# Multiplying keys by bf16 pairs on VectorE, with moved evictions and a split last zero write, in a decode-attention gradient kernel

## The chip, the cores and the metric

The kernel runs on one core of one Trainium2 chip. The metric is device time in microseconds (us) of one execution, and the figure for a kernel is the median over its runs. Engines are named as the profile names them: PE is the matrix engine, PEld its weight load, DVE the vector engine, ACT the scalar engine, POOL the GpSimd engine, and SP the engine that issues most transfers. PEclk is the clock that was granted to PE, as a share of full speed. A program on one core has no other core to compare with, so a run counts as slow only when it is more than 1.5% above the fastest run of the same kernel.

## The reference, cut to what matters

The reference is one decode step of a transformer block, forward, and the gradients of it with respect to the input, both caches and all weights. There are two sequences (B = 2), one new token each, 32 query heads on 8 key/value heads (REP = 4 query heads share one), head size 128, and caches of 32,768 rows. Attention looks at the last W = 4096 rows only.

```python
def _A_ref(x, k_cache, v_cache, wq, wo):
    ...
    W = min(4096, max(256, Sk // 4))                 # 4096 of 32768
    q = (x @ wq) ...                                 # 32 heads of 128
    k = jnp.repeat(k_cache[:, :, Sk - W:, :], rep, axis=1)
    v = jnp.repeat(v_cache[:, :, Sk - W:, :], rep, axis=1)
    scores = jnp.einsum("bhqd,bhkd->bhqk", q, k) * (Dh ** -0.5)
    p = _softmax(scores, axis=-1)
    return jnp.einsum("bhqk,bhkd->bhqd", p, v) ... @ wo

h  = x + _A_ref(_layernorm(x), ...)
h2 = h + (gelu(ln2 @ w_gate) * (ln2 @ w_up)) @ w_down      # ln2 = _layernorm(h)
# returned: h2 and the gradients for x, k_cache, v_cache, wq, wo, w_gate, w_up, w_down
```

What matters for the time: the gradients of the two caches have the caches' full shape, and 28,672 rows of each (sequence, head) are zero. These are 32 regions of 7.34 MB, 234.9 MB of zeros that have to be written. Everything else that the kernel loads and stores is 96.7 MB.

## The kernel before: the parts that count

All zero writes are issued at the start on POOL's own transfer queue, from one tile of zeros. They run behind everything else for most of the program.

```python
ZE = 1024
zt = const.tile([P, ZE], U8)
zero_regions = [o[b, g, 0:Z, :].rearrange("r d -> (r d)")
                for o in (out_2, out_3) for b in range(B) for g in range(HKV)]

def zero_cast(i):                                     # 7.34 MB, rows of 4 KB
    nper = (Z * DH // 2) // (P * ZE)
    nc.gpsimd.dma_start(out=zero_regions[i].bitcast(F32).rearrange("(p k e) -> p k e", p=P, k=nper),
                        in_=zt[:].unsqueeze(1).to_broadcast([P, nper, ZE]))
# ...
for i in range(len(zero_regions)):
    zero_cast(i)
```

`attention(b)` treats the eight heads of one sequence in turn. Its rows of keys K and values V lie on 128 partitions, 32 rows (NJ) of 128 on each. Per head it transposes K on PE and evicts the transposes from PSUM (`kt_unit`), makes the scores, the exponentials `ef` (`softmax`), and then, in eight units of four rows (`m_unit`), the products of each key row with its four exponentials. PE multiplies these products `pk` with V into `M_ps`, which the gradient of the scores needs later. `finish` copies the head's other sums out of PSUM: the copy into `oPK` on DVE marks the end of a head in the trace.

```python
def evac(out, in_):                                   # alternates DVE and ACT
    ...

def kt_unit(g, u):
    ...                                               # 8 transposes of K into KT_ps on PE
    evac(KT[:], KT_ps[:])
    return KT

def softmax(g):
    ...
    ef = stA.tile([P, NJ, REP], F32, tag="ef", name="ef")
    nc.vector.tensor_tensor(out=ef[:], in0=S[:], in1=negm[:]..., op=ALU.add)
    nc.scalar.activation(out=ef[:], in_=ef[:], func=ACT.Exp)
    Ef[g] = ef
    ...

def m_unit(g, u, M_ps):
    pk = at(PK_OFF[b][u % n_pk], [P, pk_j, REP, DH], BF16, "pK")
    ef, Kb = Ef[g], Kt[b, g]
    j0 = u * pk_j
    for (n, h0, h1) in ((pk_j, 0, 2), (pk_j - 1, 2, 3)):              # 1024 and 384 elements on DVE
        shape = [P, n, h1 - h0, DH]
        nc.vector.tensor_tensor(out=pk[:, 0:n, h0:h1, :], in0=Kb[:, j0:j0 + n, :].unsqueeze(2).to_broadcast(shape),
                                in1=ef[:, j0:j0 + n, h0:h1].unsqueeze(3).to_broadcast(shape), op=ALU.mult)
    for (jj, i) in [(jj, 3) for jj in range(pk_j)] + [(pk_j - 1, 2)]: # 5 x 128 elements on ACT
        nc.scalar.activation(out=pk[:, jj, i, :], in_=Kb[:, j0 + jj, :], func=ACT.Copy, scale=ef[:, j0 + jj, i:i + 1])
    ...                                               # oPK_ps and M_ps matmuls

def finish(g, M_ps):
    oPK = stA.tile([P, 2, DH], F32, tag="oPK", name="oPK", bufs=1)
    nc.vector.tensor_copy(out=oPK[:], in_=oPK_ps[:])
    ...
```

The order of the whole program is attention(0), the FFN and score gradients of sequence 0, attention(1), the same for sequence 1, the weight gradients, and last the tail: the used rows of the cache gradients are outer products. Each group is made by PE into `ps_g`, evicted in turn by DVE and ACT, and stored in pieces of 1 MB on SP's queue.

```python
for n, (b, what) in enumerate(jobs):                  # dV and dK of each sequence
    for gq in range(2):
        ...
        for jp in range(8):
            for ap in range(2):
                ps = ps_G.tile([P, 2, 4 * DH], F32, tag="ps_g", name="ps_g")
                ...                                   # two matmuls
                for a in range(2):
                    evac(st_vs[a][:, ap * 2:(ap + 1) * 2, :, jp, :], ps_v[:, :, a * 2:(a + 1) * 2, :])
        for a in range(2):
            for b2 in range(2):
                nc.sync.dma_start(out=dst_v[:, b, gq * 4 + a * 2 + b2, :, :], in_=sts[a][:, b2, :, :])
```

## Time and profile before

The time before is 820.84 us (five runs, 819.89 to 821.32). The span of the profiled run is 819.7 us, from its first to its last instruction.

| what | before |
|---|---|
| time, median | 820.84 us |
| DVE, ACT, PE busy over the span | 62%, 54%, 72% |
| zeros written (queue q0), everything else (q1) | 234.88 MB, 96.74 MB |
| first and last eviction of the tail | 701.2 and 806.6 us |
| last packet of zeros | 734.5 us |
| zero bytes still to write when the tail begins | 1.95 MB |

Here are lines of the profile page of the kernel before: the span, the busy time of each engine in us, its share of the span and its number of instructions; the span in 40 equal slices of 20.5 us, where a digit is the busy share of a slice in tenths and the last row is the DMA rate in GB/s; and the software queue that writes the zeros with its packets, megabytes and share.

```profile
span 819.7 us, 13311 instructions
PE 591.9 (72%) x5316; PEld 325.4 (40%) x5350; DVE 509.4 (62%) x893; ACT 443.1 (54%) x1016; POOL 35.9 (4%) x49
...
DVE  2899799603252323979484851435646637999993
ACT  1898789403333423979484731333644434576683
...
GB/s 364 415 419 420 421 422 422 423 425 423 423 423 422 418 416 426 421 421 422 423 422 424 424 423 424 423 423 422 428 416 424 425 425 427 351 295 279 387 275 341
...
q0 software_dynamic: 57856, 234.88, 86.1%
```

No engine of the core is busy all the time, and the DMA row tells why that is not the whole matter: for 33 slices (2 to 34) it stands at 415 to 428 GB/s. Only in the last six does it drop, to 351 down to 275. So the program has two parts. Up to about 697 us the transfers run flat out, whatever the compute does; after that the transfers wait for compute. The share of busy time averaged over the span says nothing about either part.

Three stretches of the table of busy time show what compute does in them. The columns are the stretch in us, its length, then the busy time and the count of each engine, the granted clock, the DMA share and the DMA rate. The first stretch is one from attention(0), the others are from the end of the tail.

```profile
core 0: us, PE busy (x) PEld busy (x) DVE busy (x) ACT busy (x) POOL busy (x), PEclk, DMA share, GB/s
41.00:61.50 20.50, 17.81 (x238) 10.62 (x239) 19.98 (x33) 20.01 (x62) 0.00 (x0) 1.00 1.18 420
758.50:779.00 20.50, 14.27 (x44) 4.76 (x45) 19.02 (x27) 12.84 (x22) 0.00 (x0) 0.84 0.93 383
779.00:799.50 20.50, 17.11 (x59) 5.69 (x59) 18.68 (x31) 16.99 (x30) 0.00 (x0) 0.99 0.67 278
```

In attention(0) DVE and ACT are both full (19.98 and 20.01 us of 20.5). In the tail DVE is nearly full with evictions and the DMA runs at 278 GB/s: it has room. What fills the two engines in attention is in the list of groups, kept apart by shape. The columns are the line, engine, operation, output and input with their sizes, the count, busy time in us, the mean of one in ns, and the idle time before them with what ended it.

```profile
L377 ACT ACTIVATE mem<-mem,ef 128x128 bf16<-128x128 bf16 x640 | 200.0, 390 | 22.1 <-PE M_ps L388 16.9 <-remote 2.4 <-ACT mem L377 1.0
L374 DVE TENSOR_TENSOR mem<-mem,ef 128x1024 bf16<-128x1024 bf16 x128 | 154.8, 1209 | 17.5 <-PE M_ps L388 17.3
L374 DVE TENSOR_TENSOR mem<-mem,ef 128x384 bf16<-128x384 bf16 x128 | 69.3, 541 | 0.0
```

The two DVE sizes give a line: (1209 - 541) / (1024 - 384) = 1.044 ns per element, and 1209 - 1024 x 1.044 leaves about 140 ns of fixed cost. The exponentials are read as 32-bit floats.

Attention(1) looks different. The chain of work that ended last is followed back from the end. These three of its lines are its longest waits for transfers (start in us, length in us, what):

```profile
388.55 29.02 DMA mem<-in_A_v_cache_dram
...
433.83 31.34 DMA mem<-in_A_v_cache_dram
...
474.84 31.37 DMA mem<-in_B_w_down_dram
```

The last heads of attention(1) wait for loads of V that land some 30 us after they are issued, and the FFN then waits for w_down.

### The profile page before, as it was taken

What the parts mean: (1) busy time and instruction counts of PE and PEld (TensorE: products, weight loads), DVE (VectorE), ACT (ScalarE), POOL (GpSimd) and SP (SyncE); (2) the same over time, 40 slices, a digit from 0 to 9 for tenths busy, and PEclk for the clock granted to TensorE, in tenths of its full rate; (3) what the DMA queues carried; (4) which work ended last, traced back from release to release, by engine and by line L of the source; (5) the groups of instructions that cost most, each with busy time, mean ns of one, the idle gap of its engine ahead of it and who ended that gap; (6) DMA issues with size and microseconds to landing.
All of it is one profiled execution on the core that took longest, in us unless ns stands there. A gap on an engine that the chain in (4) does not pass through costs nothing.

```text
span 819.7 us, 13311 instructions
## 1 busy us (share of the span) xinstructions
PE 591.9 (72%) x5316; PEld 325.4 (40%) x5350; DVE 509.4 (62%) x893; ACT 443.1 (54%) x1016; POOL 35.9 (4%) x49
## 2 busy tenths in 40 slices
PE   3787877718977845877474776887988597776682
PEld 3554443307566633444242334474433142222220
DVE  2899799603252323979484851435646637999993
ACT  1898789403333423979484731333644434576683
POOL 4100000001000000000000000000000000000000
PEclk9999999965866975989796895956965586888897
DMA  9999999999999999999999999999999999976968
GB/s 364 415 419 420 421 422 422 423 425 423 423 423 422 418 416 426 421 421 422 423 422 424 424 423 424 423 423 422 428 416 424 425 425 427 351 295 279 387 275 341
DMA packets 69462, 332.48 MB, mean 406 GB/s; under 512 B 1804, under 2 KB 1816, under 8 KB 59288
## 3 DMA queue, kind: packets, MB, share of 16 engines
q0 software_dynamic: 57856, 234.88, 86.1%
q1 hardware_dynamic: 11532, 96.74, 49.3%
q8 instruction: 42, 0.69, 0.3%
q10 hardware_dynamic: 12, 0.01, 0.2%
q14 instruction: 20, 0.16, 0.1%
HBM read 49.29 MB, written 282.33 MB: 405 GB/s over the span
## 4 chain that ended last, share of the span: by engine, by line
PE 25%; DVE 12%; DMA 11%; ACT 5%; issue 2%; ACTq 0%; DVEq 0%; SPq 0%
DMA mem<-in_A_v_cache_dram 7%; PE ps_g L774 5%; DVE mem L88 4%; ACT mem L90 4%; DMA mem<-in_B_w_down_dram 4%; PE ps_gr L665 4%; PE ps_tb L225 4%; PE VT_ps L596 3%; DVE mem L374 2%; PE dP_ps L605 2%; PE M_ps L388 2%; DVE mem L253 2%; DVE mem L685 2%; PE ps_gq L745 1%; PE d_ln_ps L722 1%
## 5 line engine op out<-in xcount | busy, mean ns | idle before, releaser
L374 DVE TENSOR_TENSOR mem<-mem,ef 128x1024 bf16<-128x1024 bf16 (+1 forms) x256 | 213.7, 875 | 17.5 <-PE M_ps L388 17.3
L377 ACT ACTIVATE mem<-mem,ef 128x128 bf16<-128x128 bf16 x640 | 200.0, 390 | 22.1 <-PE M_ps L388 16.9
L388 PE MATMUL M_ps<-mem 128*128 128x512 bf16 x498 | 139.8, 397 | 36.0 <-DVE mem L374 29.7
L90 ACT COPY mem<-ps_tb 128x512 bf16<-128x512 bf16 x83 | 48.5, 585 | 127.0 <-PE ps_tb L225 73.3
L225 PE MATMUL ps_tb<-ident_bf,mem 128*128 128x128 bf16 x664 | 81.5, 266 | 25.1 <-DMA mem<-in_B_w_down_dram 16.9
L774 PE MATMUL ps_g<-mem 128*128 128x512 bf16 x250 | 80.6, 422 | 25.7 <-ACT mem L90 23.8
L88 DVE COPY mem<-ps_tb 128x512 bf16<-128x512 bf16 x83 | 35.2, 424 | 94.6 <-PE ps_tb L225 61.1
L90 ACT CAST mem<-ps_g 128x512 bf16<-128x512 f32 x128 | 74.7, 585 | 32.2 <-DVE mem L88 30.0
L88 DVE CAST mem<-ps_g 128x512 bf16<-128x512 f32 x128 | 82.6, 687 | 8.3 <-PE ps_g L774 6.5
L388 PEld LDWEIGHTS <-mem 128*128 128x128 bf16 x512 | 42.9, 100 | 97.2 <-DVE mem L374 54.0
L225 PEld LDWEIGHTS <-mem 128*128 128x128 bf16 x664 | 55.4, 129 | 51.2 <-issue 29.2
L332 PE MATMUL KT_ps<-ident_bf,mem 128*128 128x128 bf16 x512 | 47.0, 244 | 29.9 <-DMA mem<-in_A_k_cache_dram 19.7
L90 ACT COPY mem<-KT_ps 128x1024 bf16<-128x1024 bf16 x32 | 32.0, 1001 | 58.1 <-PE KT_ps L332 58.1
L774 PEld LDWEIGHTS <-mem 128*128 128x128 bf16 x256 | 26.7, 105 | 79.0 <-issue 65.4
L104 POOL DMA_DIRECT2D out_dram<-zt x32 | 33.7, 1143 | 517.3 <-DMA out_dram<-zt 505.9
L90 ACT COPY mem<-VT_ps 128x1024 bf16<-128x1024 bf16 x33 | 34.0, 1031 | 35.2 <-PE VT_ps L596 26.7
L332 PEld LDWEIGHTS <-mem 128*128 128x128 bf16 x512 | 36.7, 109 | 41.3 <-DMA mem<-in_A_k_cache_dram 20.2
L596 PE MATMUL VT_ps<-ident_bf,mem 128*128 128x128 bf16 x512 | 47.1, 244 | 1.6 <-DVE pkT L572 0.9
L596 PEld LDWEIGHTS <-mem 128*128 128x128 bf16 x512 | 37.9, 110 | 25.0 <-issue 17.7
L382 PE MATMUL oPK_ps<-mem 128*4 128x128 bf16 x512 | 28.7, 232 | 22.8 <-DMA mem<-in_A_v_cache_dram 22.8
L605 PE MATMUL dP_ps<-mem 128*128 128x512 bf16 x114 | 41.4, 437 | 4.8 <-ACT mem L90 4.8
L88 DVE CAST mem<-ps_gr 128x512 bf16<-128x512 f32 (+1 forms) x40 | 26.7, 671 | 28.6 <-PE ps_gr L665 28.4
(196 smaller groups left out, 628.2 us busy)
## 6 DMA issues: line engine op xcount, KB each, us to landing
out_dram<-zt POOLq DMA_DIRECT2D x32, 7168.0 KB, 163.3
out_dram<-mem SPq DMA_DIRECT2D x36, 1024.0 KB, 10.1
mem<-in_A_k_cache_dram SPq DMA_DIRECT2D x16, 1024.0 KB, 17.5
mem<-in_A_v_cache_dram SPq DMA_DIRECT2D x16, 1024.0 KB, 29.2
out_dram<-mem SPq DMA_DIRECT2D x5, 1792.0 KB, 25.1
mem<-in_A_wq_dram SPq DMA_DIRECT2D x1, 4096.0 KB, 12.5
mem<-in_A_wo_dram SPq DMA_DIRECT2D x1, 4096.0 KB
mem<-in_B_w_down_dram SPq DMA_DIRECT2D x2, 1792.0 KB, 27.3
```

The source lines that it names most:

```text
L88: nc.vector.tensor_copy(out=out, in_=in_)
L90: nc.scalar.copy(out=out, in_=in_)
L104: nc.gpsimd.dma_start(out=zero_regions[i].bitcast(F32).rearrange("(p k e) -> p k e", p=P, k=nper), in_=zt[:].unsqueeze(1).to_broadcast([P, ...
L225: nc.tensor.transpose(out=ps[:, a, :], in_=src_block(a), identity=ident_bf[:])
L332: nc.tensor.transpose(out=KT_ps[:, jj, :], in_=Kt[b, g][:, u * 8 + jj, :], identity=ident_bf[:])
L374: nc.vector.tensor_tensor(out=pk[:, 0:n, h0:h1, :], in0=Kb[:, j0:j0 + n, :].unsqueeze(2).to_broadcast(shape), in1=ef[:, j0:j0 + n, h0:h1]. ...
L377: nc.scalar.activation(out=pk[:, jj, i, :], in_=Kb[:, j0 + jj, :], func=ACT.Copy, scale=ef[:, j0 + jj, i:i + 1])
L388: nc.tensor.matmul(out=M_ps[:], lhsT=Vt[b, g][:, j, :], rhs=pk[:, jj, :, :].rearrange("p i d -> p (i d)"), start=(j == 0), stop=(j == NJ - 1))
L596: nc.tensor.transpose(out=VT_ps[:, jj, :], in_=Vt[b, g][:, a * 8 + jj, :], identity=ident_bf[:])
L605: nc.tensor.matmul(out=dP_ps[:, c, :], lhsT=dOpad[:, w0:w0 + P], rhs=VT[:, c * 4:(c + 1) * 4, :].rearrange("d a k -> d (a k)"), start=(i = ...
L665: nc.tensor.matmul(out=ps[:, :n], lhsT=lhsT_fn(k), rhs=rhs_fn(k), start=True, stop=True)
L774: nc.tensor.matmul(out=ps[:, a2, :], lhsT=lhs_bf[:, jp * P:(jp + 1) * P], rhs=rhs_bd[:, ap * 2 + a2, gq * 4:(gq + 1) * 4, :].rearrange("q ...
```

## The change

The change was meant to relieve DVE and ACT in attention. It has five parts.

1. In `m_unit` four DVE multiplies of 512 elements replace the two DVE multiplies and the five ACT multiplies. The exponentials are first written as bf16, each twice, so that all three operands are bf16 and are read in pairs of neighbouring elements.
2. ACT takes all evictions of the transposed K, which DVE and ACT shared before.
3. `ef` has one buffer instead of two, and the matmuls for `oPK_ps` are done with V for all four rows, then with K.
4. Small row tiles move: a pool is removed, `x` is loaded again when needed, the residual is added by four small matmuls instead of one, and a selector exists at partition 64 too. This is left out of the diff below.
5. The last zero region is written by three transfers (116 x 3, 128 x 11 and 12 x 3 rows of 4 KB) instead of one.

```diff
+    def zero_cast4(i):
+        ch = zero_regions[i].bitcast(F32).rearrange("(c e) -> c e", e=ZE)
+        c0 = 0
+        for n, k in ((116, 3), (P, 11), (12, 3)):
+            nc.gpsimd.dma_start(out=ch[c0:c0 + n * k, :].rearrange("(p k) e -> p k e", k=k),
+                                in_=zt[0:n, :].unsqueeze(1).to_broadcast([n, k, ZE]))
+            c0 += n * k
...
     for i in range(len(zero_regions)):
-        zero_cast(i)
+        (zero_cast if i < len(zero_regions) - 1 else zero_cast4)(i)
...                                        # in kt_unit
-                evac(KT[:], KT_ps[:])
+                nc.scalar.copy(out=KT[:], in_=KT_ps[:])
...                                        # in softmax
-                ef = stA.tile([P, NJ, REP], F32, tag="ef", name="ef")
+                ef = stA.tile([P, NJ, REP], F32, tag="ef", name="ef", bufs=1)
+                ee = stA.tile([P, NJ, REP, 2], BF16, tag="ee", name="ee")
...
-                Ef[g] = ef
+                nc.vector.tensor_copy(out=ee[:], in_=ef[:].unsqueeze(3).to_broadcast([P, NJ, REP, 2]))
+                Ef[g] = ee
...                                        # in m_unit
-                for (n, h0, h1) in ((pk_j, 0, 2), (pk_j - 1, 2, 3)):
-                    shape = [P, n, h1 - h0, DH]
-                    nc.vector.tensor_tensor(out=pk[:, 0:n, h0:h1, :], in0=Kb[:, j0:j0 + n, :]..., in1=ef[...]..., op=ALU.mult)
-                for (jj, i) in [(jj, 3) for jj in range(pk_j)] + [(pk_j - 1, 2)]:
-                    nc.scalar.activation(out=pk[:, jj, i, :], in_=Kb[:, j0 + jj, :], func=ACT.Copy, scale=ef[...])
+                shape = [P, pk_j, DH // 2, 2]
+                for i in range(REP):
+                    nc.vector.tensor_tensor(out=pk[:, :, i, :].rearrange("p j (d t) -> p j d t", t=2),
+                                            in0=Kb[:, j0:j0 + pk_j, :].rearrange("p j (d t) -> p j d t", t=2),
+                                            in1=ef[:, j0:j0 + pk_j, i, :].unsqueeze(2).to_broadcast(shape), op=ALU.mult)
...                                        # oPK_ps matmuls reordered; row tiles moved
```

## The prediction

It was written before the changed kernel had run. Its text, word for word:

> **What bounds the kernel now.** Two things in turn. The page's 40 slices show DMA at 9 tenths and 415-425 GB/s until about 697 us: 235 MB of zeros (software queue, table of DMA queues) and 97 MB of loads and stores. From 697 us to the end the rate drops to 352, 295, 279, 387, 275, 341 GB/s: there the last dK/dV matmuls and their evictions (chain of waits: ps_g matmuls and evictions in turn) set the pace, and the stores wait for them. So the 332 MB need about 790 us at 421 GB/s (my estimate), and the kernel loses some 30 us because its dependent chain of compute reaches the tail too late. Shortening any stretch on that chain moves the tail forward and lets zeros fill the free bandwidth.
>
> **The attention stage on that chain.** In the table of busy time by stretches, DVE and ACT are both busy 18-20.5 of 20.5 us in most of attention(0) (20-160 us). Ends of heads (the oPK copy on DVE) lie 15.6-16.2 us apart, 20.1 and 17.2 where a K load is waited for. Per unit of four rows DVE spends 1209+541 ns (groups by form), overlapping by about 70 ns per instruction, and ACT five multiplies of 390 ns. In attention(1) the last four heads are tied to V loads instead: the chain of waits shows 29.0 and 31.3 us for V, then 31.4 us for w_down.
>
> **What the change does.**
> 1. It replaces those multiplies by four DVE multiplies of 512 elements with the exponentials stored as bf16 pairs. 1024 elements in 1209 ns and 384 in 541 ns [...]. [...] Estimate: 267+141 = 408 ns each, 340 effective, 1.36 us per unit against 1.61.
> 2. ACT loses 640 multiplies (200 us busy) and takes all K^T evictions (64 x 1.0 us): about 5 us per head, no limit.
> 3. DVE loses two K^T evictions (678 ns) per head, gains a pair-making copy (about 0.35 us): about 12.7 us per head.
> 4. PE is then the limit: 32 M matmuls at 0.217 us, 64 oPK at 0.056, transposes, scores: 13-14 us per head at full clock.
> 5. The moves of x, the small rows and the selectors, and four small residual matmuls instead of one, cost under 1 us. Splitting the last zero region changes which DMA engines carry it; worth 0-4 us at the end.
>
> **Sum.** I expect 14.2 us per head: attention(0) 13 us shorter; attention(1) 9-10 us shorter, as only heads 0-3 gain fully and the V latency stays. w_down waits stay. So the tail starts some 22 us earlier; about 11 MB of zeros then remain beside stores that need 280 GB/s, which fits. Predicted 799 us, range 790 to 812; chances: faster 0.70, same 0.28, slower 0.02.
>
> **Right or wrong if:** the multiplies show about 400 ns (right) or 675 ns ([...]DVE about 23 us per head, slower); head spacing about 14 us in attention(0); V waits of about 29 us remain in attention(1); tail evictions start near 678 us instead of 700; the last slices carry 340-420 GB/s with zeros lasting beyond 750 us.
>
> **What would make it wrong:** [...]PE throttled in the denser stage; K loads (22 us from issue to landing) becoming the limit of attention(0); stores slowed by the zeros still queued, giving the gain back at the end.

Passages are cut from it, where marked. What stays is the line of the trace: 1.044 ns per element and 141 ns. The 267 ns in the estimate of 408 ns are half of 512 x 1.044 ns: that the pairs halve the time per element was the assumption, and the 675 ns are the same line without it. No term of the sum is cut, but its gain per head rests on that assumption: 13 us in attention(0) and 9 to 10 us in attention(1) are some 22 us, and 821 - 22 gives the 799 us.

Measured beside its other figures: in the kernel before, the starts of the `M_ps` matmuls lie 0.216 us apart (45.52 to 45.95 us, granted clock 1.00), those of the `oPK_ps` matmuls come in groups of four with 0.055 us from group to group, so 0.056 us for each of the 64 was too much, and the K loads of attention(0) took 20.4 to 23.1 us to land. In the changed kernel the copy that makes the pairs took 0.29 us in the median.

## More of the kernel before

The view of waits gives what PE lost to the V loads: the sum in us, the number of waits and the longest.

```profile
PE oPK_ps L382 <- DMA mem<-in_A_v_cache_dram: 22.8, 4, 10.0
```

## The result, and the profile after

The changed kernel takes 807.63 us (eight runs, 806.38 to 807.95). The ratio is 0.9843, with a 95% interval from 0.9828 to 0.9857, so it is 1.57% faster: "same" by the 2% line. Here and below a ratio is the mean time of one kernel's fast runs over the mean of the other's fast runs of the same rounds, so it is not quite the ratio of the medians quoted. The profiled run has a span of 804.5 us, 15.2 us less than before. The mean granted clock was 0.805, and 0.817 before, so the gain did not come from the clock.

The same lines of the profile page, for the changed kernel:

```profile
span 804.5 us, 12906 instructions
PE 587.6 (73%) x5293; PEld 327.0 (41%) x5356; DVE 462.6 (58%) x1133; ACT 283.2 (35%) x408; POOL 38.6 (5%) x53
...
DVE  2698799123433208694663623456566458999970
ACT  1533230024334413240210013327544345667660
...
GB/s 364 414 421 416 421 424 422 423 425 421 423 423 420 416 421 422 421 421 423 422 422 425 425 423 422 423 423 428 416 429 422 423 423 418 420 417 417 402 406 182
...
q0 software_dynamic: 58944, 234.89, 87.5%
```

ACT's busy time fell from 443.1 to 283.2 us, and DVE's by 47 us although it now makes all the products. The DMA row is the one that decides: it no longer drops at slice 35. It stays above 400 GB/s to slice 39, and then has one slice of 182. The dip before the end has been filled, and the last slice of DVE is empty: the kernel now ends with a stretch in which only transfers run.

The groups that replaced the multiplies and took the evictions:

```profile
L392 DVE TENSOR_TENSOR mem<-mem,ee 128x512 bf16<-128x512 bf16 x512 | 181.0, 422 | 46.1 <-PE M_ps L403 46.0
...
L350 ACT COPY mem<-KT_ps 128x1024 bf16<-128x1024 bf16 x64 | 63.4, 1013 | 112.9 <-PE KT_ps L348 108.0
```

One multiply of 512 elements takes 422 ns, where the line from before gives 512 x 1.044 + 140 = 675 ns. Both stretches of the table of busy time that still have compute in them:

```profile
41.00:61.50 20.50, 19.83 (x270) 11.15 (x272) 19.58 (x63) 6.25 (x8) 0.00 (x0) 1.00 1.17 418
758.50:779.00 20.50, 17.30 (x58) 5.61 (x59) 19.25 (x31) 17.62 (x31) 0.00 (x0) 1.00 1.02 418
```

In attention(0) ACT is now idle most of the time (busy 6.25 us of 20.5), while PE and DVE are both close to full. In the tail, 758.5 to 779 us, the DMA carries 418 GB/s where it carried 383 before.

The starts of the copies into `oPK` mark the ends of the heads. They were read from the trace's order in time:

```
attention(0) before   41.7  57.9  73.7  93.8 109.5 126.7 142.3 155.4
attention(0) after    40.4  53.6  68.5  82.0 100.6 114.1 128.3 139.3
attention(1) before  336.8 355.5 372.6 388.3 415.6 433.6 461.4 477.8
attention(1) after   316.7 333.7 349.5 362.6 386.0 407.2 427.2 450.6
```

Attention(0) ends 16.1 us earlier. Attention(1), from the end of its long wait for a K load (316.7 us before, 298.6 us after) to its last head, takes 152.0 us where it took 161.1 us, 9.1 us less. Its waits for V and w_down have stayed, as the same three lines of the chain and the line of waits show:

```profile
362.75 30.89 DMA mem<-in_A_v_cache_dram
...
407.31 32.39 DMA mem<-in_A_v_cache_dram
...
448.04 31.68 DMA mem<-in_B_w_down_dram
```

```profile
PE oPK_ps L399 <- DMA mem<-in_A_v_cache_dram: 26.5, 4, 11.0
```

Then comes the account of where the gain went. All of it is from the two profiled runs:

| | before | after | difference |
|---|---|---|---|
| first eviction of the tail | 701.2 us | 674.6 us | -26.6 us |
| last eviction of the tail | 806.6 us | 780.1 us | -26.5 us |
| zero bytes left when the tail begins | 1.95 MB | 13.08 MB | |
| last packet of zeros | 734.5 us | 791.0 us | |
| from the last eviction to the end | 13.1 us | 24.4 us | +11.3 us |
| span | 819.7 us | 804.5 us | -15.2 us |

Compute finishes 26.5 us earlier. The span is only 15.2 us shorter. The rest, 11.3 us, is given back after the last eviction, where nothing but transfers runs. The 26.5 and the 11.3 us belong to this one execution, because compute also depends on when loads land: in the profile of the first experiment below, whose compute is the same, one K load of attention(0) took 32.3 us to land instead of 17.5, attention(0) ended at 150.3 us instead of 139.3, and the last eviction came at 788.9 us instead of 780.1. What the last transfers look like shows in narrow stretches of the same table, for the changed kernel (the last two columns are the DMA share and GB/s):

```profile
780.00:784.00 4.00, 0.00 (x0) 0.00 (x0) 0.00 (x0) 0.10 (x1) 0.00 (x0) 0.56 0.99 409
784.00:788.00 4.00, 0.00 (x0) 0.00 (x0) 0.00 (x0) 0.00 (x0) 0.00 (x0) 0.50 1.03 426
788.00:792.00 4.00, 0.00 (x0) 0.00 (x0) 0.00 (x0) 0.00 (x0) 0.00 (x0) 0.50 0.72 299
792.00:796.00 4.00, 0.00 (x0) 0.00 (x0) 0.00 (x0) 0.00 (x0) 0.00 (x0) 0.50 0.29 123
796.00:800.00 4.00, 0.00 (x0) 0.00 (x0) 0.00 (x0) 0.00 (x0) 0.00 (x0) 0.50 0.16 68
800.00:804.00 4.00, 0.00 (x0) 0.00 (x0) 0.00 (x0) 0.00 (x0) 0.00 (x0) 0.50 0.09 37
```

There are two things in it. First, 5.37 MB of stores are still queued at 780.1 us; at 421 GB/s they alone take 12.8 us (an estimate from these numbers). But in the kernel before 4.24 MB were left at its last eviction as well, the last four stores of 1 MB: only 1.13 MB, or 2.7 us (an estimate), is new. Stores had been waiting behind the zeros: the list of DMA issues gives each store of 1 MB a median time from issue to landing, the last number of the line. It is 10.1 us before (and 8.9 us in the changed kernel with two zero regions fewer, an experiment below),

```profile
out_dram<-mem SPq DMA_DIRECT2D x36, 1024.0 KB, 10.1
```

and 20.3 us after.

```profile
out_dram<-mem SPq DMA_DIRECT2D x36, 1024.0 KB, 20.3
```

Second, the rate does not fall from 420 to nothing: it falls from 426 to 299, 123, 68 and 37 GB/s. Sixteen engines carry about 421 GB/s, so one carries 26 to 27, and 123 GB/s is the work of about five engines, 37 of one or two. The packets in flight agree: 16 up to 788 us, 5 at about 792, 3 at about 797, 1 at 802. After 790 us only 1.44 MB moved, which sixteen engines would have carried in 3.4 us (an estimate), ending near 793. The last packet landed at 803.2 us. So some 10 us of the end are the work of a few engines that lag behind the others. In the kernel before the last packet landed at 817.8 us, 1.1 us after the end that the same estimate gives. Most of the 11.3 us is therefore the lag, and not the amount.

### The profile page after: what moved, and what is told of

Its sections match the earlier page's. It is cut to its first block, busy times and chain, and to the rows that moved or that the text cites. A ratio compares the mean times of both kernels' runs of the same rounds, so it can differ in the third digit from the quotient of the medians.

```text
span 804.5 us, 12906 instructions
## 1 busy us (share of the span) xinstructions
PE 587.6 (73%) x5293; PEld 327.0 (41%) x5356; DVE 462.6 (58%) x1133; ACT 283.2 (35%) x408; POOL 38.6 (5%) x53
## 4 chain that ended last, share of the span: by engine, by line
PE 38%; DMA 18%; DVE 13%; ACT 9%; issue 4%; ACTq 0%; DVEq 0%; SPq 0%
DMA mem<-in_A_v_cache_dram 8%; ACT mem L90 8%; DMA mem<-in_B_w_down_dram 7%; PE ps_tb L241 7%; PE ps_g L791 5%; DVE mem L88 4%; PE M_ps L403 4%; PE VT_ps L612 4%; PE ps_gr L682 4%; PE dP_ps L621 3%; DVE mem L392 3%; DMA mem<-in_A_k_cache_dram 3%; PE d_ln_ps L550 2%; DVE mem L269 2%; PE KT_ps L348 1%
## 5 line engine op out<-in xcount | busy, mean ns | idle before, releaser
L392 DVE TENSOR_TENSOR mem<-mem,ee 128x512 bf16<-128x512 bf16 x512 | 181.0, 422 | 46.1 <-PE M_ps L403 46.0
L403 PE MATMUL M_ps<-mem 128*128 128x512 bf16 x469 | 139.8, 400 | 12.7 <-DVE mem L392 9.1
L350 ACT COPY mem<-KT_ps 128x1024 bf16<-128x1024 bf16 x64 | 63.4, 1013 | 112.9 <-PE KT_ps L348 108.0
L399 PE MATMUL oPK_ps<-mem 128*4 128x128 bf16 x1024 | 33.8, 235 | 28.8 <-DMA mem<-in_A_v_cache_dram 26.5
L612 PEld LDWEIGHTS <-mem 128*128 128x128 bf16 x512 | 38.1, 111 | 25.1 <-issue 17.9
L682 PE MATMUL ps_gr<-mem 2*128 2x512 bf16 (+1 forms) x78 | 32.7, 506 | 14.8 <-DVE mem L702 7.6
## 6 DMA issues: line engine op xcount, KB each, us to landing
out_dram<-mem SPq DMA_DIRECT2D x36, 1024.0 KB, 20.3
```

What stands on the lines that cost most here:

```text
L350: nc.scalar.copy(out=KT[:], in_=KT_ps[:])
L392: nc.vector.tensor_tensor(out=pk[:, :, i, :].rearrange("p j (d t) -> p j d t", t=2), in0=Kb[:, j0:j0 + pk_j, :].rearrange("p j (d t) -> p ...
L399: nc.tensor.matmul(out=oPK_ps[32 * c:32 * c + REP, a, :], lhsT=eT[:, j % 8, j // 8, g * REP:(g + 1) * REP], rhs=src[:, j, :], start=(j < 4 ...
L403: nc.tensor.matmul(out=M_ps[:], lhsT=Vt[b, g][:, j, :], rhs=pk[:, jj, :, :].rearrange("p i d -> p (i d)"), start=(j == 0), stop=(j == NJ - 1))
L612: nc.tensor.transpose(out=VT_ps[:, jj, :], in_=Vt[b, g][:, a * 8 + jj, :], identity=ident_bf[:])
L682: nc.tensor.matmul(out=ps[:, :n], lhsT=lhsT_fn(k), rhs=rhs_fn(k), start=True, stop=True)
```

## The experiments

The theory after this comparison was: (a) the gain comes from attention alone, and in it from the faster multiply (422 ns) and the evictions moved from DVE; (b) the kernel is now bound by the transfers queued behind the zeros, so that a part of the gain is lost at its end. The rivals were that the split of the last region or the moved rows give the gain, that PE and not DVE sets the pace of a head, and that the tail is still bound by evictions. Twelve kernels were run. All were timed against the kernel before in the same rounds, except two that were given one look.

### The last zero region in one transfer (changed kernel)

```diff
-        (zero_cast if i < len(zero_regions) - 1 else zero_cast4)(i)
+        zero_cast(i)
```

> The changed kernel, but the last zero region is written by one DMA as in the kernel before. Profile of the changed kernel: compute ends at 781 us of the span, the other DMA engines run dry at 790, and the stores land until 803 at 127 falling to 33 GB/s, which is the rate of few engines. Theory A (the split takes load off lagging engines): without it the last stores land later, total 809 to 814 us. Rival B (the 116- and 12-partition pieces fall on few engines and make the lag): total 797 to 804 us. Neither, if within 2 us of 807.6.

It took 809.92 us, 0.9863 of the time before [0.9848, 0.9878]. By the medians the split is worth 2.3 us, but the interval overlaps that of the changed kernel, so it is not resolved whether it is worth anything. The end of it looks different, though. Here are its last stretches:

```profile
792.00:796.00 4.00, 0.00 (x0) 0.00 (x0) 0.00 (x0) 0.00 (x0) 0.00 (x0) 0.50 1.01 420
796.00:800.00 4.00, 0.00 (x0) 0.00 (x0) 0.00 (x0) 0.00 (x0) 0.00 (x0) 0.50 0.80 334
800.00:804.00 4.00, 0.00 (x0) 0.00 (x0) 0.00 (x0) 0.00 (x0) 0.00 (x0) 0.50 0.06 27
804.00:808.00 4.00, 0.00 (x0) 0.00 (x0) 0.00 (x0) 0.00 (x0) 0.00 (x0) 0.50 0.04 14
```

Without the split all engines but one are done at about 800 us, and exactly one works on at 27 GB/s to 806 us. The same was seen of the zeros: from 726 us to the last packet of zeros at 762 us, one engine alone still had any. So one engine ends some 6 us behind the other fifteen even without the split. With the split there are about five laggards instead of one. The changed kernel's queue of zeros has 1,088 packets more than before, nearly all of 4 bytes, and their number fits a piece of 116 x 3 rows that landed on four engines only, 87 rows on each. That explains four of the five by the count of packets; it was not seen engine by engine.

### The split alone (kernel before)

```diff
-        zero_cast(i)
+        (zero_cast if i < len(zero_regions) - 1 else zero_cast4)(i)
```

> The kernel before with only the split of the last zero region added. In the kernel before the last store group is issued at 806-809 us and compute sets the end, so both theories expect 819 to 822 us, no gain beyond 0.3%: the attention change then carries the whole gain. If the split alone carried a good part of the 13 us, it would be below 816 us.

It took 820.6 us, a ratio of 0.9994 [0.9977, 1.0011]. In the kernel before the zeros are over 72 us before the last eviction, so how they end can't matter. By itself the split brings nothing.

### Two zero regions fewer, in both kernels (wrong results on purpose)

```diff
-    for i in range(len(zero_regions)):
+    for i in [*range(len(zero_regions) - 3), len(zero_regions) - 1]:
```

These two kernels leave 14.7 MB of the output unwritten. They ask each kernel whether it is bound by bytes.

> Wrong on purpose: the changed kernel without two of the 32 zero regions (14.7 MB, 35 us at 421 GB/s). Theory A (queued bytes, with lagging engines, set the end of the changed kernel): the end moves to the end of compute, 781 us, plus about 9 us for the last store group as in the kernel before: total 790 to 795 us. Rival (compute still sets the end): within 3 us of 807.6.

> Wrong on purpose: the kernel before without the same two zero regions. Its tail is set by compute from about 700 us on, so taking 35 us of DMA work away should bring at most 4 us: 817 to 821 us. The gap to the changed kernel without them should then be the full compute gain of 25 to 29 us. If the kernel before is bound by bytes, it falls by 20 us or more.

The changed kernel with two regions fewer took 785.36 us (782.8 to 787.59), 0.9562 of the time before. The kernel before with two regions fewer took 820.92 us, a ratio of 0.9991 [0.9974, 1.0008]. So 14.7 MB less are worth 22 us in the changed kernel and nothing in the one before. The changed kernel is bound by its transfers, the one before by its compute. Without the last of the zeros the changed kernel's lead is 820.92 - 785.36 = 35.6 us, more than the expectation of 25 to 29 us. In this profile compute also ended 7.4 us earlier than in that of the changed kernel, at 772.7 us: its waits for V in attention(1) summed to 17.2 us instead of 26.5.

The end of it looks like the end of the kernel before: the DMA has room again (384 GB/s), and it follows the compute. The stretches of the changed kernel with two regions fewer are

```profile
758.50:779.00 20.50, 11.14 (x38) 3.44 (x36) 12.66 (x20) 12.31 (x21) 0.00 (x0) 0.85 0.93 384
779.00:799.50 20.50, 0.00 (x0) 0.00 (x0) 0.00 (x0) 0.00 (x0) 0.00 (x0) 0.78 0.19 79
```

and the time from its last eviction (772.7 us) to its end is 12.9 us, against 13.1 us before and 24.4 us in the changed kernel. With two regions fewer the lagging engines cost nothing.

### The old attention in the changed kernel

```diff
-                nc.scalar.copy(out=KT[:], in_=KT_ps[:])
+                evac(KT[:], KT_ps[:])
...          # ef/ee, the multiplies and the order of the oPK_ps matmuls as before the change
```

> The changed kernel with the attention stage of the kernel before (multiplies on DVE and ACT with f32 exponentials, K^T evictions shared); the moved rows, selectors and the split zero region stay. If the attention stage carries the whole gain, 819 to 823 us. If the moves or the split carry part of it, below 816 us.

It took 820.5 us, where the kernel before took 822.09 us in the same rounds, a ratio of 0.9987 [0.9966, 1.0007]. The moved rows and the split, kept here, give nothing that can be told from zero. The whole gain comes from attention. Of its parts, the pairs and the evictions are tested next; the single buffer of `ef` and the order of the `oPK_ps` matmuls were not tried apart.

### The multiplies on 32-bit exponentials

```diff
-                ee = stA.tile([P, NJ, REP, 2], BF16, tag="ee", name="ee")
-                nc.vector.tensor_copy(out=ee[:], in_=...)
...
-                                            in1=ef[:, j0:j0 + pk_j, i, :].unsqueeze(2).to_broadcast(shape), op=ALU.mult)
+                                            in1=ef[:, j0:j0 + pk_j, i].unsqueeze(2).to_broadcast(shape), op=ALU.mult)
```

> The changed kernel with its four DVE multiplies of 512 elements, but with the exponentials in f32, so not all operands are 2-byte. [...]one multiply rises from 422 ns to about 675 ns, DVE needs about 22 us per head, attention(0) ends some 60 us later, and the total is 860 to 920 us. If the speed came from the shape or from leaving ACT alone, the multiply stays near 422 ns and the total near 807 us.

The group of its multiplies, by shape:

```profile
L390 DVE TENSOR_TENSOR mem<-mem,ef 128x512 bf16<-128x512 bf16 x512 | 316.4, 680 | 39.6 <-PE M_ps L400 39.6
```

The same 512 elements take 680 ns when one operand is 32 bits wide, and 422 ns when all are bf16. The heads end 21 to 23 us apart instead of 13 to 15, except where a load is waited for and at the last head (19.6 us). Three of its four runs, the profiled one among them, were slow, so its median of 913.42 us is not compared with anything. The evictions of `ps_g` on DVE take 687 ns in this profile as in that of the kernel before. Its one fast run took 898.73 us. That is 9% above the 822.09 us of the kernel before in the same rounds: four DVE multiplies in place of two and five ACT ones are a large loss without the pairs, and a gain with them. The difference, 680 - 422 = 258 ns, is close to half of 512 x 1.044 = 535 ns: between these two kernels the time per element is about halved. They differ in two things, the type of the exponentials and their reading in pairs, and which of the two counts was not tried apart.

### The K^T evictions shared again

```diff
-                nc.scalar.copy(out=KT[:], in_=KT_ps[:])
+                evac(KT[:], KT_ps[:])
```

> The changed kernel with the K^T evictions shared by DVE and ACT again, the multiplies as changed. DVE gets 2 x 0.68 us per head back and stands at about 14 us, level with PE, so compute ends 3 to 10 us later than 781 us. Since DMA ends 22 us after compute in the changed kernel, that should be hidden: total within 3 us of 807.6. If compute still sets the end, 811 to 818 us.

It took 815.69 us (814.52 to 819.12), a ratio of 0.9941 [0.9911, 0.997]. This expectation missed: the change was thought to vanish behind the transfers, and it cost 8 us against the changed kernel. Two evictions of 684 ns came back to DVE per head, 1.37 us, and the heads of attention(0) that wait for nothing ended 14.6 us apart instead of 13.2 us. The stretch of it in attention(0):

```profile
41.00:61.50 20.50, 18.14 (x250) 10.99 (x254) 19.84 (x60) 4.42 (x6) 0.00 (x0) 1.00 1.19 425
```

What DVE got, the head took, to the tenth of a microsecond, while PE's busy time fell from 19.83 to 18.14 us of the 20.5. So it is DVE, not PE, that sets the pace of a head after the change. The reason why it could not vanish is that the last eviction moved from 780.1 to 800.8 us, much further than the 3 to 10 us that had been estimated. Sixteen heads times 1.4 us are 22 us (an estimate), but not all of the shift is shown to come from there: a K load took 31.8 us to land here too, and in the run with one plain transfer such a load went with a shift of 8.8 us without any change in compute. With that the kernel is bound by compute again, and ends 12.5 us after its last eviction.

### Zeros taken from one engine

The next four kernels, three of them deals of a few pieces and one of many, ask whether the lagging end can be mended by dealing the last zero region out unevenly. What the traces show of a deal is a count of packets. In the kernel before, the 32 zero transfers have 57,344 packets of 4 KB and 512 of 4 bytes, sixteen for each transfer; the changed kernel has 1,600 of 4 bytes. The 1,088 more fit a deal (an estimate) in which each transfer brings sixteen, and an engine that is left out of a piece gets as many packets of 4 bytes as another gets rows: 12 x 87 + 16 for 116 x 3 rows on four engines, and 4 x 3 + 16 for 12 x 3 rows on twelve. No packet carries an engine number, so which engines a piece goes to is not shown.

```diff
-        for n, k in ((116, 3), (P, 11), (12, 3)):
+        for n, k in ((120, 10), (112, 5), (32, 1)):      # 120 rows: meant for 15 engines
```

> The changed kernel with another split of the last zero region: 120 partitions x 10, 112 x 5 and 32 x 1 rows. [...] In the run with one plain DMA exactly one engine had zeros left from 725 to 761 us and stores left from 799 to 806 us. If that is the sixteenth engine and its lag sets the end, the total falls to 795 to 801 us. If another engine lags, or the pieces are dealt out otherwise, 806 to 814 us.

The piece of 120 was meant to leave out one engine, called the sixteenth, and so to spare it 80 rows (0.33 MB, 12 us at 27 GB/s, an estimate). The page counts 57,968 packets on the zero queue, 112 more than before. Two transfers more bring 32 of them, and the other 80 fit one engine left out.

```diff
-        for n, k in ((116, 3), (P, 11), (12, 3)):
+        for n, k in ((8, 1), (120, 10), (9, 8), (P, 4)): # the same, aimed at another engine
```

> The changed kernel with a third split of the last zero region: 8 x 1, 120 x 10, 9 x 8 and 128 x 4 rows. What the runs so far showed: the 116 x 3 and 12 x 3 pieces brought 1088 extra packets of 4 bytes, which is 12 x 87 + 16 plus 4 x 3 + 16, so 116 partitions were dealt to four engines and 12 to twelve; 120 x 10 brought 96, which is 1 x 80 + 16, so one engine got none. [...] If the eighth engine is the one that lags, its end moves 11 us forward, and the total falls to 796 to 801 us. If it is another engine, the total is 808 to 812 us, as in the run with one plain DMA.

This deal was meant to leave one engine, called the eighth, 41 rows, and the others 113 to 120.

The two kernels took 810.32 us (0.9863 [0.9848, 0.9878]) and 810.67 us (0.9861 [0.9844, 0.9877]): no better than the last region in one transfer. The end of the first of them shows why; these are its last stretches:

```profile
796.00:800.00 4.00, 0.00 (x0) 0.00 (x0) 0.00 (x0) 0.00 (x0) 0.00 (x0) 0.50 0.07 29
800.00:804.00 4.00, 0.00 (x0) 0.00 (x0) 0.00 (x0) 0.00 (x0) 0.00 (x0) 0.50 0.06 27
804.00:808.00 4.00, 0.00 (x0) 0.00 (x0) 0.00 (x0) 0.00 (x0) 0.00 (x0) 0.50 0.05 23
```

One engine works alone from 796 to 807 us. The compute of this profile ended at 772.5 us, 7.6 us before that of the changed kernel, and it did not help at all: the end came 36.2 us after the last eviction. So here the time is set by the slowest engine and not by compute. Neither deal shortened the lag. No run here names the lagging engine, so it is not shown whether either deal spared it.

### Zeros dealt in graded pieces

```diff
+    SMALL = (17, 17, 17, 17, 17, 31, 47, 17, 61, 71, 89, 103, 109, 127, 139, 17)
+    # 16 transfers from one partition each, of so many rows, issued between the earlier regions
...
+    # the rest of the last region: 128 x 7 rows
```

> A measurement of which DMA engine lags, not an improvement. Half of the last zero region is written by sixteen DMAs of a prime number of 4 KB rows[...]; the other half goes evenly to all. With 56 rows for each from the even half, the rows are 73 73 73 73 73 87 103 73 117 127 145 159 165 183 195 73 in the order of issue, against 112 with one plain DMA. A row takes 0.15 us at 27 GB/s. With the plain DMA the lagging engine ended its stores at 805.4 us and the others near 793. So it should now end near 799.5 (73 rows), 801.6 (87), 804 (103), 806 (117), 808 (127), 810 (145), 812.5 (159), 813.4 (165), 816 (183) or 818 us (195), and each of the others near 793 plus the same shift. If 8 x 17 tiny packets or another deal of rows shows instead, the engine stays unnamed. Total 801 to 822 us.

This was to give every engine a different load, so that the end would name the laggard; that each piece goes to one engine, the next piece to the next, was an assumption. It took 811.13 us and named nothing. It was run at another time. The number of tiny packets speaks against one engine for each piece. Beside its 57,344 rows of 4 KB the zero queue has 912 packets of 4 bytes. One per engine for each of the 48 transfers are 768. The other 144 are the number that sixteen equal shares, rounded up, lack over the sixteen pieces (for 17 rows, 32 - 17 = 15); one engine for each piece would, by the count that fits the other deals, have brought 15 times 896, or 13,440. So the count fits pieces that were spread over all sixteen engines, and the experiment is inconclusive.

### Zeros taken from five engines

```diff
-        for n, k in ((116, 3), (P, 11), (12, 3)):
+        for n, k in ((4, 109), (5, 19), (7, 107), (P, 4)):
```

> The changed kernel with the last zero region in pieces of 4 x 109, 5 x 19, 7 x 107 and 128 x 4 rows. [...] A row takes 0.15 us. If the lagging one is among the five, it ends near 797 us and the others near 797: total 798 to 802 us, with 496+1324+225+979+16 = 3040 packets of 4 bytes. If it is another engine, its end moves 4 us back: total 812 to 817 us. If the pieces are dealt out otherwise, the count of 4-byte packets differs.

This kernel took 815.81 us (812.07 to 816.85), 0.9923 of the time before, 8 us worse than the changed kernel. The count of the deal came out as expected: the page has 60,384 packets on the zero queue, which are 57,344 rows and 3,040 packets of 4 bytes, the number worked out beforehand for pieces on four, five, seven and sixteen engines. But the end did not. These are stretches of its table:

```profile
779.00:799.50 20.50, 0.00 (x0) 0.00 (x0) 0.00 (x0) 0.00 (x0) 0.00 (x0) 0.50 0.90 364
799.50:820.00 20.50, 0.00 (x0) 0.00 (x0) 0.00 (x0) 0.00 (x0) 0.00 (x0) 0.57 0.14 55
```

Two to four engines were still at work after 800 us (55 GB/s over the slice), and the end came 47.2 us after the last eviction. By intention five engines were spared 61 rows, 0.25 MB each, and the other eleven got 27 or 29 rows more. Either the laggard was not among the five, or what the eleven got made new laggards of them. The theory that the laggards are known well enough to be spared has fallen. Which engine lags, and why, stays open. One candidate was a queue that fetches instructions: it moves 42 packets, 0.69 MB, on top of the rest. If a single engine carried all of it, at 27 GB/s it would fall 25 us behind (an estimate), which is of the order of the 36 us for which one engine alone still had zeros to write. The kept traces speak against it. In five profiles (the changed kernel, the plain transfer, the two deals aimed at one engine, the graded pieces) a fetch of 16 KB falls into the time when one engine alone still writes zeros, at 775.2, 733.2, 766.6, 774.1 and 773.0 us. The zeros of that engine go on through it, one packet every 0.51 us at most, where they come every 0.47 us without it; a fetch of 16 KB at 27 GB/s would hold them up for 0.6 us (an estimate). So these fetches did not run on the lagging engine. The trace with the plain transfer also shows that the lag grows long before the tail: from 497 to 569 us the last of the sixteen engines completes a region every 17.9 to 18.2 us, and the first every 17.2 to 17.3 us.

### One zero region only (wrong result)

```diff
-    for i in range(len(zero_regions)):
+    for i in [len(zero_regions) - 1]:
```

> Wrong on purpose: the changed kernel with only the last of the 32 zero regions. Theory: the 25 to 32 us between the issue of a V or w_down load and its landing is time behind the zero stream, not the load's own 4-5 us of data. Without the stream the loads land within 10 us of issue, the waits for V in attention(1) (26 us in sum) are gone, those for w_down (15 and 32 us) shrink to under 10 each, and the total falls to 690 to 740 us. Rival (the loads themselves are slow): the waits stay and the total stays above 765 us, near the 772 us at which compute ended without two regions.

It took 697.29 us, with its last eviction at 682.9 us. It was run at another time. Lines of its page and its only waits of PE for a cache load:

```profile
GB/s 356 416 419 420 249 21 108 205 8 61 1 2 118 244 184 12 113 62 88 97 33 74 1 1 2 1 146 98 107 105 106 1 152 97 258 400 279 265 380 345
```

```profile
PE KT_ps L348 <- DMA mem<-in_A_k_cache_dram: 1.4, 2, 0.9
```

The view of a tensor (`--tile in_A_v_cache_dram`) gives the time from issue to landing of the four V loads that are issued during attention(1). In the kernel before (`--window 370:470`) it was

```profile
DMA to landing us min/median/max: 29.0/29.3/31.3
```

and without the zeros (`--window 296:365`)

```profile
DMA to landing us min/median/max: 4.9/4.9/5.0
```

In the changed kernel, with all its zeros, it was 22.9 to 32.4 us. Without the zeros no wait for V or w_down is left, and the heads of both attentions end 12.7 to 13.5 us apart, with one gap of 14.5 us and 11 us at the last of each. So the 30 us of a V load are not the load: they come with the zeros. In the kernel before, the data packets of the V load issued at 388.55 us ran from 398.9 to 403.3 us, while its sixteen completions landed between 404.8 and 417.6 us, all but one by 410.6 us. The last completion alone added 7 us to this load. Why the data started only 10 us after the issue, and why the completions came up to 14 us after the data, is not shown. The run also sets the two bounds of this kernel apart: compute alone needs some 697 us, the transfers alone need 332.5 MB / 421 GB/s = 790 us (an estimate).

No kernel of the study that writes the whole result is faster than the changed one.

## Why the prediction was right and where it was wrong

The time, 807.63 us, lies in the predicted range of 790 to 812 us, 8.6 us above the predicted 799. The chance of 0.70 was put on faster by over 2%, and it was 1.57%: "same", which had 0.28. That the time came so close is in part luck: compute gained 4.5 us more than predicted, and 11.3 us were lost in a term that the sum did not have.

**The multiply: right.** The prediction gave 408 ns and 340 effective, on the assumption that the pairs halve the time per element. The trace shows 422 ns, and 16 multiplies in a row in 5.46 us, so 341 ns effective. It does so although the two elements of a pair are the same number and the row of pairs is read again and again. With 32-bit exponentials it was 680 ns.

**Attention on the critical path: right, and a little too small.** Predicted were 14.2 us per head, 13 us off attention(0) and 9 to 10 us off attention(1). Measured were 13.2 us for a head that waits for nothing and 14.1 us on average, 16.1 us and 9.1 us. (The 13.2 us recur in the other profiles of this attention code; the 16.1 us are of this execution, and would be 5.1 us in the profile with one plain transfer.) The V waits of about 29 us stayed, as predicted. The tail was to begin some 22 us earlier, near 678 us; it began 26.6 us earlier, at 674.6 us.

**"PE is then the limit": wrong.** The prediction put DVE at 12.7 us per head and PE at 13 to 14. When 1.37 us of work was given back to DVE, a head took 1.4 us more and PE's busy time fell. DVE still set the pace. The step had no weight in the sum, but it made the expectation for the shared evictions wrong.

**The last zero region: right, as far as it goes.** Predicted were 0 to 4 us at the end; 2.3 us were found, with intervals that overlap. In the kernel before it is worth nothing.

**"About 11 MB of zeros then remain beside stores that need 280 GB/s, which fits": this is the step that failed.** The amount was nearly right (13.08 MB), and slices 35 to 39 carried 402 to 420 GB/s, as foretold. But the prediction compared means: bytes left over the mean rate of sixteen engines. Stores queue behind zeros (10.1 us from issue to landing became 20.3 us), 5.37 MB of them were still to move when compute had ended (4.24 MB before), and the program ends with its slowest engine, not with the mean: the last packet landed 10 us after the time at which sixteen equal engines would have been done. The span from the last eviction to the end grew from 13.1 to 24.4 us, and 11.3 of the 26.5 us were lost there. The prediction did name "stores slowed by the zeros still queued, giving the gain back at the end" among what could make it wrong, and gave it no number. In the sum it reads: -26.5 us at the last eviction instead of -22, and +11.3 us after it instead of nothing.

That the transfers, not the evictions, bind the changed kernel is shown by the pair with two regions fewer (22 us against 0), and by the five ways in which the last region was dealt out in timed runs: compute ended between 767.6 and 788.9 us in their profiles, and the end did not follow it (814.8 us for the earliest, 808.0 us for the latest). That one or a few engines finish late is seen in the profile of the changed kernel and in those of all five other deals of its last region. Which engine, and why it is behind, is not known.

## What to carry to other kernels

When a kernel has a queue of background transfers, compare two finish lines before costing a change: the one of the dependent chain, and the one of the bytes, and take for the latter the slowest DMA engine and not the mean rate. Here the first stood at 820 us and the second at some 805 us (the mean rate alone gave 790), and compute that ended 26.5 us earlier brought 15 us. On DVE, a broadcast operand that is stored as bf16 pairs can turn a multiply of 680 ns into one of 422 ns, which can be worth more than sharing the work with another engine.
